# A new issue order for an H3 convolution and MLP kernel: the same operations, moved in three stretches

## The chip, the cores and the metric

The kernel runs on one core of one Trainium2 chip. The metric is the device time of one execution in microseconds (us). A core has a tensor engine (PE), a vector engine (DVE), a scalar engine (ACT), GpSimd (POOL) and a sync engine (SP). Each engine works through its own list of instructions in order and waits on semaphores for what the others deliver. SP and POOL start DMA transfers here: SP nearly all of the plain loads and stores, and POOL the transfers that add what they bring to what is already at their destination.

## What is computed

Two layers are applied twice, each on a normalised input and added back to it. Layer A is an H3 convolution, layer B a two-matrix MLP with ReLU (S = 2048, D = 640, Dff = 1728, batch 1):

```python
def A(q, k, v, shift_k, ssm_k, ssm_D):
    kv = causal_depthwise_conv4(k, shift_k) * v
    y  = irfft(rfft(pad(kv)) * rfft(pad(ssm_k)))[:S] + kv * ssm_D
    return q * y
def B(x, w1, w2):
    return maximum(x @ w1, 0) @ w2
x = q
x = x + A(layernorm(x), k, v, ...);  x = x + B(layernorm(x), w1, w2)
x = x + A(layernorm(x), k, v, ...);  x = x + B(layernorm(x), w1, w2)
```

The convolution depends on k and v alone, so both rounds multiply by the same y. The kernel computes y once, stores it in device memory (`Y`) and loads it when a gate needs it.

## The kernel before, in words

The sequence is cut into 8 chunks of 256 positions and the channels into 5 tiles of 128. A convolution **unit** `c_t` is chunk `c` of channel tile `t` (tile names carry it: `gt4_2` belongs to unit 4_2). For each unit the shift convolution is built on ACT and DVE (`tp`, `acc`), transformed blockwise on PE, and gives two spectra: `at`, that of the input, and `gt`, that of the filter. The output of a unit is a sum of products of spectra over pairs of chunks (`products`, L713): DVE multiplies `Ax` or `at` by `Gx` or `gt` into `pd` (L761) and adds it to `pacc` (L766); the sum is combined to `u` (L798 to L801), split into a high and a low half-precision part (`hlu`, L405), transformed back on PE (`pq`, L383 to L385) and stored as `Y`. Spectra that later units need are written to device memory (stores `A<-at` and `G<-gt`, L701) and loaded again as `Ax` and `Gx` (L748) into a ring of six buffers.

A spectrum has three parts; the third is the sum of the first two. From chunk 4 on that sum is made by a transfer instead of an engine: POOL starts a DMA that adds part 1 onto part 2's copy. A copy on ACT (L629 for `gt`, L670 for `at`) comes ahead of it. The same is done for the folded filter `gs` = `hf` plus or minus `hr`:

```python
def psum_(x):                                                    # L624
    plan.op("POOL", 1.1, lambda: POOL.dma_start(out=x[:, :, 2],
            in_=x[:, :, 1], accum_op=ALU.add), [x], [x], ...)    # L626
...
plan.op("POOL", 1.1, lambda g=g: POOL.dma_start(out=g.t,
        in_=hr.t, accum_op=ALU.add), [hr, g], [g], ...)          # L501
```

The text calls these forty transfers the **adding transfers**, and those of L626 a unit's **sum**. A filter's way to PE is `gs`, then its split `hlg` (L405), then the matmuls `pg` (L383 to L385).

Between the convolution's pieces runs the MLP, whose matmuls fill most of PE's time: `h` (L1319 to L1334) against the first matrix, then the split `hh` (ACT, L1470) and `hl` (DVE, L1471), then `o` and `oc` (L1303 to L1306) against the second. An `h` tile is in PSUM, and its buffer is free for the next one when `hl` has been written from it.

What is written in the program is only which operations exist and what they need. The order in which they are issued is a list, the table `ORDER` (L60 to L163): 4073 numbers packed into text, one per operation. `table` (L283) unpacks it and `issue` (L286) emits the operations in just that order; each engine's instruction list is that list cut down to its own operations. A tile takes a buffer of its ring when its first operation is issued, and waits for the buffer's last user. So the table sets three things at once: the order on each engine, the order in the DMA queues, and which buffer a tile gets.

Of the kernel before, what the change touches and what calls it, by code (L numbers as in the profile page):

```python
# [59 lines left out]
ORDER = (  # L60
    "0{{d71po#B2LK2F2>=QJ3jhoN4FC=R4*(DV5dabZ695zd6#y0h7XTOl82}mp8vq;t9RMBx9{?Z#Apjx(BLE}-B>*M>Cjck_DF7+}"
    "D*!A20st)lE&wk8FaR+CG5|9GGyquuRsdH300031Q2;dnHUKvOH~={SIsiKWJODiaJ^()eKmb7iLI6VmL;ytqMgT_uNB~IyN&rg$"
    "k^oWwTmV=ATL4S|O#n^+PXJH=S^#DMT>xnSU;thKX8>OSVE|$PmH?LkXaH&easYDxV*r={lK_+eQvjI&WB_ykbpUn%cK~<*c>sC<"
    "WdLjddjOgMn*e+OeE@y{e*l00YXFr1gaCm6f&ha6zyP5DZ2*P<ZUCGBg#g3=!2oaoB>{&3!T=`$ZvZI)D*>bcodBKyp8%i$#Q??t"
    "#{kFxaR4m=!vLZHqX4A<F99Y2hyaNIiU249tpKM0t^lt9u>hz5%K*#(&H&E<rU0@4$pDK0i~!95vjFM<sQ`@t$^fbW(Eus|ECH(k"
    "&;YmqtN_vgxd1T%GXd}bH36^y(*TYD*8q<Iv;f!u*#O%B+yFNLE&(tBG66IJ)c`pG?f}#PwE(sNI{`fbkpPeYHUZrL>;Sv~?*Q5W"
    ")&REvKLNe~;{d$?-T)8*NdXc8H~~5VK><7g;s8DY-vI3Z5dlj969E(f`~VdJO#v1G;Q&toKmkGl^8nxg<^W0o7XcmtQ31aIQvpK("
    "=Kxg!7y(xS83E`3L;?K({s2V*SpgaWTLJL^OabWtP60*%0RjI20s%(>9RWxIAps%*Z2?^YPyr(WBmsp1@&I}PZUKe?QUQkni2;fM"
    "ive%}i~(N(0|8V4Zvk-uasgHWSOJXz1OZ_IjsbH4b^-PPbODb6V*%>`djVPjTmg3hhyi>7cma6<UIAbMzX6c}x&V*?egS;}Vgd93"
    "lL5d1_W*wZ!2!DfWC6kfWdV`_#Q|mk!vSXjXaRx(!~tmmlmUPN#sO*p%K^**#{tLzl>vbPmjQzTmI2WLnE}!Pm;v<w$pM4`$^p#*"  # L70
    "r2@_Y@&Ts;fCAG2g94fXoB{Iz^a1q&)B&FX8v&aEodKZ%paG)+o&op)`2nc{_yD2-<N(hB&;j`X_5o`F_W`8=009L7qyeS@`T!*Y"
    "`T>Xn`vLm^rvV%R`~m#|*8$i8r~#<~i2@)2s{yJ32LXfv0s^c7*#X`G+5xQr+X00Fh5`ryuK}(Bs{+*l0|KxC)&aQ!hXRWN;Q`_S"
    "2?1;Y1_9gwu>pz#vH{%zi~?)|-vQtOr~<PAv;pS<=mFya<p2r+jsm&@jRFe+wE?yPj{>&=xB=w>kOH{@=>e1i3;}@xx&i6|w*uq="
    "*aGGOy8)E~mjeC)bpe(F4gtLZkpjE{k^;T~>j9Gj>;dfo?g4@U9|5KU4FT@~{{ip;00IF5m;wX>xB{vI@c{(_CIXoPCjtfnz5*x$"
    "oC2K!2m(|9tOD8s3IZttDgp-r2?DzURREd-3j(bIzyd4+Edrhb4FcQ(y#l`i3<3`VpaKvA4g#M7n*uHZ-U1N<t^zLtFaj|G!UD$v"
    "!2%Kj6ao(cp#l{G69TXT!veelD*_q<7y>c^5d*{mu>!9G76LN@qXM!5q5|py#RA&`8v+>u$pSS3HUhH(7Xrot69XOs9|AW590Ifg"
    "@dC91-vT%S$O7;J$^sn%wgMmm-2&|b%K{++&jL9D%mUd0Is(lCA_Cw7&;ro{VFc^~BLdO_;R53VKLR@fJOb_lBmzJJ<O0(I)B^7U"
    "K>{BGJp$qa{{rO#WCUgeZ31orZvr?3J_6MO&H_RLLjrID<^n|m6a(`D@&fb%>jH5Ca{_b%^#V%*Y6Kwz=K^&C=mO~ib^`VS5(9Sv"
    "cmhlUL;^+v_X0-(00RO80|QM0P69{*0Ru?_1Oqt)c>+oT6$2In{Q@=w_yQvXQ36i_QUZDc`2wQ^R0353Bm;Z`7XwoQAOjc!{sLP9"
    "83R}X1p`n5`T|)3`vP17eFD}3A_HdxB?AWoCIcq}8Uy?SegawoT>>Zr1_NRQ8v|hie*$F$2m>htJ_KR{UIJqTDg!J790OJYR{|>o"  # L80
    "2?II=LIXPl9RptiU;+vQV*+FXJOn)iEdwtD3<E<09s_6ur34EDFas_FF#}}+4Fe7XX#_+AMFU0yqylCFKLkMprvy&~Gy-b`NCQ9w"
    "X98#fX#z3>Py|N<Hv~xoGXrb{Gy`e^LIgDfHUm)vL<B_yP6Ma}QUpo^O9Mj$Mg&I$PXki~Py<l|OaoK{Hv<p@djwSjRs(GWdIUHF"
    "O#@N`O$1j1NCa8~TLY>DR0K{0R|Hc7cm!1hZUjjLIs;q-T?1hQIRjn;Vgoz_Rs>1}aspTbWCITaSpz-;d<1?3s|0TZO9VRuOayTR"
    "Km&3FWdm3QSp;wda|BuhW&>vfqy(-6c?4erfCOLzbOfdZfdqpDe*}aCV*_XdKLcq4b_6{Gf&_I0g#?BKY6FJ^*8+$Hbpv(-eFS#|"
    "sRVlhTLfGLT?DWMi3E=Xkpyc3UIdB+kOX%F#RPZ*YXfWptOR)jlLU(dj0AcEk_3$eZUdAAl>~1C_ylbOtpu?IuLR8ma077z#{@wG"
    "js$xHnFMkJngq}Ud;{A9eFL%t%LH=+vjqACfdl*mn*_!Lf&+sCgadyAfCGmE$ON1OmITZM&IJ7g{{+tjeglmIhy#TK(FD^3mju!T"
    "m;}@WkOKe(v;@fnkpr~^)daQ#h68W~i35rQjsv#@ivyknxCFTb`2@NIj{~~|z64(codlNyU<8x{l>>|e0R?mek^|NR$^-)imIK!W"
    "m;<~7+yuV_8U@${*#w^ia|N9PlLP()1qHnX`vd|7o&(+l-vplnzy!er-2~tSpabCqn*-tmoCBEyb_L@Er~|13ssrQ%cm<#YcLnAI"
    "+60;d!vwAa!UTB*uLG+Cp#!V~1O)~Kq66gw=LC8M=met$tpmgaqXV!5v;%tuA_NBo2nDqRu>%PO3I*E)=>%~F3kB)~qywb`rUQHh"
    "?gX|2as}%Iw*w3Xx&yldrvuyr4F&83r3LQ<rv<zN4h4P%e+AtG-UFcovIBGl@C3aB4+Rhfzyq@bs0FG8!vlQ<!2{m|-~)gK!~^jJ"  # L90
    "fd#1rxC6oi;sX%{xdXlf#{+@|;{&S&tOeu)$OFFv%mvB=q6EbQ#sh-|^90EQ&I9cPqy-)Y<pbse=L2;G&;t_%=mQi5hXu<6rUkAA"
    "(F5rN>jM%6gaxk!u?5Tn6$P*b>;ugM90l?O&jZo}tp(Hri3N%Uiv`mIvIX=6^#rp876pt2)dSW8hy~XJwFT`1?gNbljs=ee&IRuS"
    "g$0oX^#d0Lw*}Y(*#rLt)di3R+5_+d@dFqIk_EN}@&f?|BLwyX)CKbclLaIM^aCXXCItHf_XGF?`2(~C0R$%mDFopI0tEU4Dg=}T"
    "D+K%l%>@Gn)&&CuECjd(*98Ow1P1*B{sS!pE(8Yzh6VQo1qLq!nFR_22m}cPFa-Yt00avJ1q9gz1_llU2L>_(xdplf&jkhq5d;qe"
# [14 lines left out]
    "wg>D7(FURhDF~wm-3PY^-Uqk`xd$T%p$4c1C<x#O_y?v2rv~2#CJ3np;RpE#(gvgkzXr?(?gym?tOouEDhMkG)CT_t00^oEs|GCy"
    ";s*f;0tmVXE(p~IO$bZ~`UiIiEC~Gt(*{lm0|*2Ntp=_J1_-YPum<A?<p<;ku?7bS1qcWT3J9_WvjzzWv<5H;MhLYA3kcQ*wg%=0"  # L110
    "5C;qhdI;AB*aq1K4G0eiF9_NOd<ahnQ3w$S5(nD`69?P|PzZkr-3I#yQV1~!6bBUtG6+WqQwR<S;06!~eF)wL;s!Mc;|4Pby9c}n"
    "5eO0pSqMl7Gzc~b-v)UI;Rb;S76%jvHwYI8fC%UY<OWFydk7N<cnCNMS_o7Kp$HELRR~H5gb1k!83%$0IS4ukeh3u^<pvfA=?3No"
# [1621 lines left out]
```

## Time and profile before

| what | value |
|---|---|
| runs of the kernel before | 844.4 us median (841.74, 844.4, 845.06) |
| the profiled execution | 844.9 us, of which the span of its trace is 843.1 us |
| PE busy | 832.4 us (99%) at full granted clock in every slice |
| DVE busy | 775.8 us (92%) |
| ACT busy | 605.1 us (72%) |
| POOL busy | 45.9 us (5%) |
| plain transfers (queue q1) | 170.47 MB |
| adding transfers (queue q0) | 10.49 MB |

All times within the execution count from the start of the span. A row of the timeline gives the start, the length, the engine and line, the operation with its output and inputs, and in brackets the idle time of the engine before it and what ended that. For an instruction that only starts a transfer (DMA_DIRECT2D) the length is the time that the engine spent on starting it, waits for earlier data included; when the data landed stands in the DMA views. "PEclk" is the clock that PE was granted, 1.00 being full speed.

### The profile page before, as it was taken

How to read it: one execution, taken by the hardware profiler on the slowest of the kernel's cores; microseconds unless marked ns; L12 is line 12 of the kernel's file. 1: busy time of each engine (PE TensorE's matmuls, PEld its weight loads, DVE VectorE, ACT ScalarE, POOL GpSimd, SP SyncE). 2: the span in 40 equal slices, each digit the busy share in tenths (PEclk: the TensorE clock that was granted, in tenths of full speed). 3: DMA queues.
4: the chain of work that ended last, by engine and by line, in shares of the span. 5: the costliest groups of instructions: out<-in, count | busy, mean ns of one | idle time of the engine just before them, and what ended most of it. 6: DMA issues, size and time to landing. Idle time of an engine off the chain costs nothing.

```text
span 843.1 us, 20661 instructions
## 1 busy us (share of the span) xinstructions
PE 832.4 (99%) x8135; PEld 660.5 (78%) x8135; DVE 775.8 (92%) x1404; ACT 605.1 (72%) x1505; POOL 45.9 (5%) x58
## 2 busy tenths in 40 slices
...
GB/s 288 339 282 326 231 176 277 291 248 311 296 282 200 272 192 225 251 257 252 196 265 204 234 259 237 220 191 228 319 243 297 116 229 139 63 68 23 58 33 32
DMA packets 138435, 182.37 MB, mean 216 GB/s; under 512 B 53857, under 2 KB 95713, under 8 KB 138338
## 3 DMA queue, kind: packets, MB, share of 16 engines
q1 hardware_dynamic: 129874, 170.47, 65.8%
q0 software_dynamic: 8320, 10.49, 8.1%
...
q10 hardware_dynamic: 144, 0.10, 0.0%
...
## 4 chain that ended last, share of the span: by engine, by line
PE 84%; DVE 6%; DMA 4%; issue 3%; ACT 2%; POOL 0%; DVEq 0%; SPq 0%; POOLq 0%; ACTq 0%
PE o L1249 10%; PE h L1331 9%; PE h L1334 9%; PE h L1332 9%; PE o L1304 7%; PE o L1303 7%; PE o L1306 6%; PE h L1319 4%; DMA gt<-gt 3%; PE pg L585 2%; PE h L1321 2%; DVE pd L761 2%; PE oc L1303 2%; PE h L1364 2%; PE hs L1364 2%
## 5 line engine op out<-in xcount | busy, mean ns | idle before, releaser
L1331 PE MATMUL h<-xT,w 128*128 128x256 f16 (+1 forms) x1000 | 229.1, 249 | 0.0
L1334 PE MATMUL h<-xT,w 128*128 128x256 f16 (+1 forms) x1000 | 229.1, 249 | 0.0
L1332 PE MATMUL h<-xT,w 128*128 128x256 f16 (+1 forms) x1000 | 229.1, 249 | 0.0
L1304 PE MATMUL o<-w,hh 128*128 128x512 f16 x336 | 127.4, 379 | 0.0
L1303 PE MATMUL o<-w,hh 128*128 128x512 f16 x336 | 127.3, 379 | 0.0
L766 DVE TENSOR_TENSOR pacc<-pacc,pd 128x1536 f32<-128x1536 f32 (+1 forms) x75 | 123.1, 1641 | 0.2
L1332 PEld LDWEIGHTS <-w 128*128 128x128 f16 x1100 | 107.6, 98 | 15.2 <-issue 0.2
L1331 PEld LDWEIGHTS <-w 128*128 128x128 f16 x1100 | 107.6, 98 | 14.9 <-DVE hh L1471 0.2
L1334 PEld LDWEIGHTS <-w 128*128 128x128 f16 x1000 | 97.8, 98 | 6.4
L1303 PEld LDWEIGHTS <-hh 128*128 128x128 f16 x672 | 65.7, 98 | 26.2 <-DVE hh L1493 0.6
L1304 PEld LDWEIGHTS <-hh 128*128 128x128 f16 x672 | 65.7, 98 | 26.1
L1306 PE MATMUL o<-w,hl 128*128 128x512 f16 x208 | 78.8, 379 | 0.0
L761 DVE TENSOR_TENSOR pd<-Ax,Gx 128x768 f32<-128x768 f32 x83 | 78.0, 949 | 0.3 <-DMA Gx<-G 0.2
L1303 PE MATMUL oc<-w,hh 128*128 128x128 f16 x336 | 73.6, 219 | 0.1
L1304 PE MATMUL oc<-w,hh 128*128 128x128 f16 x336 | 73.6, 219 | 0.0
L1470 ACT ACTIVATE hh<-h 128x512 f16<-128x512 f32 (+1 forms) x97 | 46.2, 482 | 35.0 <-PE h L1334 16.7
L1306 PEld LDWEIGHTS <-hl 128*128 128x128 f16 x416 | 40.7, 98 | 26.4 <-DVE hl L1471 1.7
L1319 PE MATMUL h<-xT,w 128*128 128x256 f16 (+1 forms) x400 | 57.6, 251 | 0.0
L479 ACT ACTIVATE tp<-kt,shs 128x256 f32<-128x256 f32 (+1 forms) x78 | 43.5, 574 | 6.9 <-DVE acc L553 6.8
L1306 PE MATMUL oc<-w,hl 128*128 128x128 f16 x208 | 45.6, 219 | 1.6 <-DVE hl L1471 1.6
L761 DVE TENSOR_TENSOR pd<-at,Gx 128x768 f32<-128x768 f32 x46 | 42.9, 948 | 0.7 <-DMA at<-at 0.6
L501 POOL DMA_DIRECT2D gs<-hr x20 | 18.5, 924 | 408.2 <-DVE pacc L766 224.6
...
## 6 DMA issues: line engine op xcount, KB each, us to landing
...
G<-gt SPq DMA_DIRECT2D x14, 768.0 KB, 5.8
A<-at SPq DMA_DIRECT2D x14, 768.0 KB, 7.2
...
gs<-in_hF SPq DMA_DIRECT2D x20, 256.0 KB, 3.7
```

What stands on the lines that cost most here:

```text
L479: ACT.activation(o[:, i : i + m], kview(i, m, j), AF.Copy, scale=shs[:, t, j : j + 1])
L761: ew(f"mac{j % POOLMOD}", 768, lambda e, x=dst[i], av=av, gv=gv: e.tensor_mul(x.t, av(), gv()), [ax, gx], [dst[i]], pr_)
L766: dve(768 * (hi - lo), lambda lo=lo, hi=hi, pd=pd: DVE.tensor_add(acc[:, lo:hi], acc[:, lo:hi], pd[:, lo:hi]), [*sums[lo:hi], *dst[lo:hi]] ...
L1249: PE.matmul(b[:, c : c + w], x, y[:, z : z + w], start=done[i] == 1, stop=end, skip_group_check=fin)
L1303: PE.matmul(z, hh[:, c], wh[:, d], start=(j == JS[0] and i == 0 and (h == 0 or s == S[0])), stop=False)
L1304: PE.matmul(z, hh[:, c], wl[:, d], start=False, stop=end and tail)
L1306: PE.matmul(z, hl[:, c], wh[:, d], start=False, stop=end)
L1319: PE.matmul(p[:, z], wh, xv(t, x), start=b and x == 0, stop=e and x == 1)
L1331: PE.matmul(p[:, z], wh, xv(t, 0), start=b, stop=False)
L1332: PE.matmul(p[:, z], wh, xv(t, 1), start=False, stop=tail and e)
L1334: PE.matmul(p[:, z], wl, xv(t, 0), start=False, stop=e)
L1470: act(2 * R, lambda pv_=pv_, hh=hh: ACT.activation(hh.t, pv_(), AF.Relu), [src], [hh], URGENT)
```

## The change

Only the table `ORDER` is replaced. The operations, their sizes, their buffers and the program around them stay as they were. The diff is two pieces of packed text, of which a line shows nothing:

```diff
 ORDER = (
-    "0{{d71po#B2LK2F2>=QJ3jhoN4FC=R4*(DV5dabZ695zd6#y0h7XTOl82}mp8vq;t9RMBx9{?Z#Apjx(BLE}-B>*M>Cjck_DF7+}"
...
```

Laid against the trace of before, operations trade places in three stretches: from the start to about 200 us, from about 312 to 385 us, and from about 400 to 484 us. Elsewhere the lists are the same. On PE 782 of 1059 operations keep their place, on DVE 899 of 1330, on ACT 718 of 1130, on SP 330 of 512 and on POOL 40 of 42. No PE operation moves by more than 14 places. Rows of the lists follow; the number behind the last underscore of a name only tells tiles of one name apart.

**SP around the store of unit 4_1's `at`** (314 to 335 us of before). This store reads what the sum of `at4_1` writes, so it and all that stands behind it wait for that sum. Before:

```order
L701 DMA A4_0_142<-at4_0_5047 128x1536
L701 DMA A4_1_144<-at4_1_5624 128x1536
L465 DMA hr4_3_5951<-in_hR 128x2x256
L861 DMA Y4_74<-ys4_0_5841 128x4x128
L498 DMA gs04_3_5991<-in_hF 128x2x256
L748 DMA Gx4_2_3_2_5993<-G3_1_137 128x768
L748 DMA Ax4_2_2_2_6004<-A2_1_134 128x768
L748 DMA Gx4_2_2_2_6037<-G2_1_133 128x768
L465 DMA vt4_3_6048<-in_vT 128x2x256
L1113 DMA y3_1_00_6052<-Y2_73 128x640
L701 DMA G4_1_143<-gt4_1_5367 128x1536
```

Now:

```order
L701 DMA A4_0_142<-at4_0_5047 128x1536
L465 DMA hr4_3_5887<-in_hR 128x2x256
L1113 DMA y2_1_01_5892<-Y2_73 128x640
L748 DMA Gx4_2_3_2_5942<-G3_1_137 128x768
L465 DMA vt4_3_5964<-in_vT 128x2x256
L861 DMA Y4_74<-ys4_0_5861 128x4x128
L748 DMA Ax4_2_2_2_5998<-A2_1_134 128x768
L748 DMA Gx4_2_2_2_6056<-G2_1_133 128x768
L498 DMA gs04_3_6087<-in_hF 128x2x256
L701 DMA A4_1_144<-at4_1_5624 128x1536
L748 DMA Ax4_2_3_2_6155<-A3_1_138 128x768
L465 DMA kt4_4_6198<-in_kT 128x2x262
```

The store of `at4_1` stands eight places further back among SP's transfers; the loads of `hr4_3`, `y`, `Gx` and `vt4_3` no longer stand behind it. The next two rows now are the load of `gs14_3` and the store of `gt4_1`.

**DVE around the first products with the sum of `gt4_2`** (341.7 to 349 us of before). Before:

```order
L557 TENSOR_TENSOR acc4_3_5775<-acc4_3_5775,vt4_3_6048 128x512
L761 TENSOR_TENSOR pd4_2_2_6099<-Ax4_2_1_2_5798,Gx4_2_3_2_5993 128x768
L761 TENSOR_TENSOR pacc4_2_6101<-Ax4_2_0_2_5795,gt4_2_5959 128x768 x2
L561 TENSOR_TENSOR sd4_3_6104<-acc4_3_5775 128x256
L1479 SCALAR_TENSOR_TENSOR hl9_6_6106<-h9_6_6007,hh9_6_6081 128x256
L761 TENSOR_TENSOR pd4_2_4_6108<-Ax4_2_2_2_6004,Gx4_2_2_2_6037 128x768
L761 TENSOR_TENSOR pd4_2_2_6099<-Ax4_2_1_2_5798,gt4_2_5959 128x768
```

Now:

```order
L801 TENSOR_TENSOR u14_1_6089<-u14_1_6089,pacc4_1_5592 128x512
L761 TENSOR_TENSOR pd4_2_2_6096<-Ax4_2_1_2_5865,Gx4_2_3_2_5942 128x768
L761 TENSOR_TENSOR pd4_2_4_6098<-Ax4_2_2_2_5998,Gx4_2_2_2_6056 128x768
L761 TENSOR_TENSOR pacc4_2_6101<-Ax4_2_0_2_5789,gt4_2_5962 128x768
L1479 SCALAR_TENSOR_TENSOR hl9_6_6103<-h9_6_6016,hh9_6_6083 128x256
L761 TENSOR_TENSOR pd4_2_2_6096<-Ax4_2_1_2_5865,gt4_2_5962 128x768
L761 TENSOR_TENSOR pd4_2_4_6098<-Ax4_2_2_2_5998,Gx4_2_3_2_5942 128x768
```

A second product of loaded tiles (`pd4_2_4`) now stands ahead of the first product with `gt4_2`. Further ahead, out of these rows, `hl9_2` has gone from two operations before the pair that writes `gt4_2` (L622, L623) to four behind it, and the two `hlg` splits of unit 4_2 stand ahead of `hl9_1`.

**POOL, the last rows before the sum of `gt6_0`** (440 us of before). Before:

```order
L626 DMA gt4_4_6983<-gt4_4_6983 128x2x256
L501 DMA gs16_0_7172<-hr6_0_6920 128x512
L626 DMA at4_4_7150<-at4_4_7150 128x2x256
L501 DMA gs06_1_7463<-hr6_1_7330 128x512
L626 DMA gt6_0_7414<-gt6_0_7414 128x2x256
```

Now:

```order
L626 DMA gt4_4_6983<-gt4_4_6983 128x2x256
L501 DMA gs16_0_7129<-hr6_0_6920 128x512
L626 DMA at4_4_7157<-at4_4_7157 128x2x256
L626 DMA gt6_0_7360<-gt6_0_7360 128x2x256
L501 DMA gs06_1_7437<-hr6_1_7521 128x512
```

The sum of `gt6_0` and the addition for `gs06_1` have changed places. In the same stretch SP's load of `vt6_2` moved from behind the store of `at4_4` (L701) and the load of `Ax6_0_3_0` to ahead of both; on DVE the product of `Ax6_0_1_0` and `Gx6_0_5_0` now stands ahead of the first product with `gt6_0`. In the opening stretch the load of `hf0_0` went from first on SP to behind `kt0_2` and the two of `kt0_0`, and the store of `gt0_0` from SP's row 49 to row 67, with its reloads right behind.

More of the change, by code (lines that the diff above doesn't have):

```diff
@@ L66 @@
[L66 to L75, printed above, removed]
@@ L91 @@
-    "fd#1rxC6oi;sX%{xdXlf#{+@|;{&S&tOeu)$OFFv%mvB=q6EbQ#sh-|^90EQ&I9cPqy-)Y<pbse=L2;G&;t_%=mQi5hXu<6rUkAA"
+    "0{{d71po#B2LK2F2>=QJ3jhoN4FC=R4*(DV5dabZ695zd6#y0h7XTOl82}mp8vv33R{#J2RsdT7T>x1C0RT||S^!c2TmS+98~_~v"
+    "U;thKVE|$PSO8xD9snNzAOIl%A^;-*BmgA<CIBY@C;%w{DgY}0EC4M4E&wk8FaR+CG5|9GGypXKHUKvOH~={SV*ok;I{-WYJpeuc"
+    "KL9`gK>$JkLjaZlL;z+0MF2(sM*v6wNdQU!O8{p8X#ivZWdLdblK^M{YyeCEO#n^+PXJH=asYDxbO3b#b^vz(cmR0-dH{O>d;pgK"
+    "eE@y{e*lyKm;h4%gaDZUl>nLmYXHCi!2pH;B>{i{n*f{uodBKyfdFj)!~n$r#sGx?hX8^Ag8;_>Cjo8%Zvb!rp#X6Jp8&`J$pFd#"
@@ new lines @@
+    "!T_WIq5z-(!vH1$tpKF}qW~!ZD*=cAt^kPurvNPhr~rxpuK=+CvH-IHC;=}4rT{Sk%K(c2&Hyt3sQ|bD%mBFn&j8H;s{o7u&;Y6c"
+    "tN^e8*8tc6(E!;1+W?IKjsPkF+yJxy>HyLJ?f|s_wg9&Pj{qzI-2l@7?*KIckN~^@y#V6?E&<g5Faa_F+5j{GHUZQC-T*fNH~~2U"
+    "Isxzi)&LLzI|1wf5djhb69GK|KLPCkNdZd%;s8MbJORD{J^|kV6af|iO#$ElPXSQ@;Q&AZ`~c<v@c=>rQvnqLzW^5j7y&~8L;*zs"
+    "=l~u8839HCRRQM!Apu7L9RWxIg#rBl8UacHOabx${s1BY=>S&&SpkOuBLV*aTLFdvi2-c^Bmr&#0Rf5uive!|0s)NyT>%3DUjd8("
+    "Z~+7XdI4bpaRG7xdjVqsjsZ>qPytc_Q~_22SOHoA9079ybODF~b^(t8Tme)7cmZAkU;%dlzX4(ac>#O@WC4%?egVJ%kpaO0!U5|5"
@@ new lines @@
+    "e*t9y^8k_oW&vjblL2S}eF13!#R0<s#sT&K!~uW-#{p^ql>vhSlmW{D$N_-?_W+jx%mJ1Gm;ucJ&H>Q@(gC{wg8`WVngN6XoB{Lz"
+    "^#FhZ(*el=)B&FX$^jbzodNOzpaB2@1p)W~p#h=+o&oa#^a1q&_5q^-r2_Z?f&%ve`2m{&r2(V?`2eQ@&jHW@rvm%|`T^Gg{Q;%{"
+    "AOZRSfdcyh`v9o{r~w86hyvIFssV`t2LY=A+5zMM2mt~DtO2b7uL0Qs+W~|Et^w5n2?5~&-T|-yYXJ%Yg#uLoB?4>#ivj}zu>s!!"
+    "h60BI-~r+RvH^+$bpieX3jwnMv;pG*)&blB-2t@$rUK*v{{gxJ<pH(<w*lq>xB(0S4FS3UjsoWai~^4WjRNHWxdFQYx&e>^kpch$"
+    "y#eR}=>h5iyaB!ew*r&`sRFA4r~;A#l>+Mlz5?t4?E&rqmjc)V+5!Or?*Z@ulL7<+m;!79@d1_s1p=G`CITk{tO5oCnF6>1f&nN3"
@@ new lines @@
+    "3IZttssfz?2LdVrzyb&Yo&v1`xdJQ#paPKqEdmPy4FV1Vy#fybt^x@H4+0DVp8^pA4gs(NE&|*FngTBZFai_;p#l{Gy8_+<u>ueR"
+    "5&{teF#;0;uL7F_zXCD>76Kmu+X5>BqXNPLvH}+Z!2-hqyaJ*E8Uix{H3Ay~#{x70HUhH(!~(Sfv;xHfHv$|2I0794>H-)783M)v"
+    "9s&~s$pW?l*#h4JVFc|0-2xv1$O6g&%L2>-AOi3LAp$u9&jLCEI|4ic&;sBB%>p6<@dDujKLXJL(*ivLBLXA>;{xOYJ_0}j(gNZF"
+    "<pM<l@&auFZUXEAK?2kQZvsXFLIO(y)dC*_<^uBqZ~|lmaRNsIa{@yG&H_vV>jD%5=K}QtAp>Rv?gB&t^aB3^bOPuCbpikb?*euL"
+    "Y6La}=>m5G0s{jBBLhtWNCNf(_X2nV5(7>G6$5z!76SnTNdig&IRy9uBm?~ddIA^&Q36r|1Orn7R08<|PXbi}qyl^bSONtDSppyf"
@@ new lines @@
+    "S^|9n`T`;Y7Xw=Y1_NONVgeZh`vMvRB?Be{{sJchTmt+8egb6#8v|zqC<7}4I0Rw@2LlKLT>?-7DFapl9RpqhR{~=MLIYm{U;;V>"
+    "WddUYJOrZz90O(oDg!J7F9R(DFatgWI|K;>3Il%vLjyeoXao!cL<24ZF#}`*K?FYpdIZ)23j+-Ur35kqMFTSfKm-m0L<DIBPXuQI"
+    "XaXJsX#z$ALIg(xNCQv=QUq!OHv}{TNdr*?Qv|03Lj*+xdjw7cPXjdrYXmj}Mg&I$Oan>-Z3IgLO#@H^NCXfAcm#X|4+B&KQ3Fi`"
+    "Hv?J&I0I4xRRdH6P6TWOT?1YNIRjGzZUj~XIs;n+R|Kd8sswKYSOa+kR|81|fCO;_aspffRRnSbRs>1}egtF#I|EAuqy(k}WdnZ%"
+    "Spz-;JOf_?Oay}jVFO|Va0IIaV*_RbU;}*wX9HLSSp<XxfdqmCa|CDuS_EqXt^{fWYXd+7bOdz+h6INMJp;%DKLd6Ibp)^kTLfGL"
@@ new lines @@
+    "g#>#7hy<(zX#;Kpkpyf5T?B~)b_2x(cLR?EcmsI@cLb>fUIcFgkOYzhiUi99lmv?eu>{QoZ3C|aa08VDaRaRcdjr=3lLVOr_yl?b"
+    "d;>uPvIKGij0E}weFJ_2%mjf0a|40{`~=PfjRcMangq}Ue*=I6vjm3&{RD#pmITiP#{`4}(FB_WjRS=P(*(%`(gd6YkOR~Nkpqqc"
+    "v;>y~hy%3*#sr-Nh6B|E)&#Z$j{~;^xCDs<iUX7bivx@Ul>@m1m<0a>+ywpvU<957x&)U4*94XWy9A#E00jXB`2@TK*aUC|ode1Q"
+    "k^^4^m;=59*#rXxo&%Eu`vkuP1qI#&-vr<Uy#${FpaXLSnF9g^;RL`0cm;U{+XHb0r~|13sso?|!35$2bOW0M-2~bMas`?LqXn)5"
+    "b_I6@1_i<d!vwDb;{>Y%+XUtW<OG}pp#!1=tOI%l#02F8umk4=dj$jqu>%JMA_NEp=mhBmd<CNe2?eAB3Iz)Vv;(yR3<aeHtpn}^"
```

55 lines of the change are left out of this document (19 added, 36 removed).

## The prediction

> **What bounds the kernel now.** I read the busy times by stretch first. The columns are the stretch, its length, the busy time of PE, PEld, DVE, ACT and POOL with instruction counts, PE's clock, DMA share and GB/s.
>
> ```profile
> 2.00:100.00 98.00, 98.00 (x1019) 83.79 (x1020) 89.09 (x197) 73.79 (x169) 0.43 (x4) 1.00 0.90 299
> 100.00:200.00 100.00, 99.96 (x1178) 80.73 (x1176) 98.14 (x178) 74.90 (x203) 0.00 (x0) 1.00 0.81 261
> 340.00:360.00 20.00, 18.36 (x152) 13.02 (x150) 17.94 (x25) 15.85 (x41) 2.06 (x2) 1.00 0.96 250
> 440.00:460.00 20.00, 16.89 (x140) 11.79 (x139) 15.90 (x25) 14.23 (x37) 3.31 (x3) 1.00 0.78 210
> 460.00:660.00 200.00, 200.00 (x1687) 149.99 (x1686) 196.28 (x285) 137.33 (x344) 15.05 (x14) 1.00 0.85 238
> ```
>
> PE sets the time: from 2 us on it is full, at full clock, except for two gaps. An order list cannot shrink PE's own work, so only the gaps can be won. PE's timeline places them (start, length, what ran, idle time ahead and what ended it):
>
> ```profile
> 357.45 0.22 PE L1303 MATMUL oc<-w,hh 128*128 128x128 f16 x1
> 357.51 0.22 PE L1304 MATMUL oc<-w,hh 128*128 128x128 f16 x1
> 359.30 0.23 PE L1306 MATMUL oc<-w,hl 128*128 128x128 f16 x1 [1.57 <-DVE hl L1471]
> ...
> 452.87 0.38 PE L1304 MATMUL o<-w,hh 128*128 128x512 f16 x1
> 453.08 0.38 PE L1306 MATMUL o<-w,hl 128*128 128x512 f16 x1
> 454.27 0.27 PE L383 MATMUL pq<-hlu,cM 128*128 128x256 f16 x1 [0.80 <-ACT at L670]
> 456.84 0.27 PE L384 MATMUL pq<-hlu,cM 128*128 128x256 f16 x1 [2.30 <-DVE hlu L405]
> 456.95 0.27 PE L385 MATMUL pq<-hlu,cM 128*128 128x256 f16 x1
> ```
>
> Counted from start to start, against the pitch of the same matmuls beside them (0.06, 0.21 and 0.11 us), the first gap costs 1.79 - 0.06 = 1.73 us, the second 1.19 - 0.21 and 2.57 - 0.11, together 3.44. The sum is 5.17 us.
>
> DVE was late in both places, and its timeline says why:
>
> ```profile
> 325.55 0.96 DVE L761 TENSOR_TENSOR pd<-at,Gx 128x768 f32<-128x768 f32 x1 [0.64 <-DMA at<-at]
> ...
> 332.72 0.69 DVE L1471 SCALAR_TENSOR_TENSOR hl<-h,hh 128x512 f16<-128x512 f32 x1
> ...
> 342.31 0.95 DVE L761 TENSOR_TENSOR pd<-Ax,Gx 128x768 f32<-128x768 f32 x1
> 345.25 1.82 DVE L761 TENSOR_TENSOR pacc<-Ax,gt 128x768 f32<-128x768 f32 x2 [2.00 <-DMA gt<-gt]
> ...
> 446.19 0.67 DVE L1471 SCALAR_TENSOR_TENSOR hl<-h,hh 128x512 f16<-128x512 f32 x1
> 450.97 0.96 DVE L761 TENSOR_TENSOR pacc<-Ax,gt 128x768 f32<-128x768 f32 x1 [4.10 <-issue]
> ```
>
> It stood still for a unit's sum: 0.64 us for `at4_1`, 2.00 for `gt4_2`, 4.10 for `gt6_0` ("issue" names nothing, but the product reads `gt`). POOL's rows give the issues, the DMA views of windows that hold an issue the time to landing (last number), and the bytes by queue (q1 plain, q0 adding):
>
> ```profile
> 315.84 1.20 POOL L626 DMA_DIRECT2D at<-at  x1 [9.26 <-ACT at L670]
> 336.54 1.21 POOL L626 DMA_DIRECT2D gt<-gt  x1 [19.50 <-ACT gt L629]
> ```
>
> ```profile
> 435.65 0.92 POOL L501 DMA_DIRECT2D gs<-hr  x1 [14.20 <-DMA Ax<-A]
> 440.61 1.20 POOL L626 DMA_DIRECT2D gt<-gt  x1 [4.04 <-ACT gt L629]
> ```
>
> ```profile
> q1 hardware_dynamic: 613, 1.45, 91.7%
> ...
> gt<-gt POOLq DMA_DIRECT2D x1, 256.0 KB, 8.7
> ```
>
> ```profile
> q1 hardware_dynamic: 700, 1.31, 87.2%
> q0 software_dynamic: 12, 0.01, 1.6%
> ...
> A<-at SPq DMA_DIRECT2D x1, 768.0 KB, 8.8
> ...
> gt<-gt POOLq DMA_DIRECT2D x1, 256.0 KB, 10.3
> ```
>
> The first of these two views is 336.5 to 341 us: no byte of an adding transfer in 4.5 us, though the sum was issued at its start. The second is 440.6 to 446. Behind a plain backlog a sum thus takes 8.7 to 10.3 us. With none it takes 4.2:
>
> ```profile
> gt<-gt POOLq DMA_DIRECT2D x1, 256.0 KB, 4.2
> ```
>
> (issued at 299.76). Landing plus nothing gives the DVE starts: 336.54 + 8.7 = 345.2, 440.61 + 10.3 = 450.9.
>
> **The change part by part.** *The second wait* (-3.44). `gt6_0`'s sum now goes ahead of the addition for `gs06_1`, whose row is above; it can start some 0.6 us sooner with the ACT copy that moved up. DVE's first product with it moves back by one `pd<-Ax,Gx` (0.87 us by pitch), and without the idle time comes near 447.3 to 447.7. On SP:
>
> ```profile
> 441.79 0.38 SPq L701 DMA_DIRECT2D A<-at  x1
> 442.23 0.53 SPq L748 DMA_DIRECT2D Ax<-A  x1
> ...
> 461.92 0.49 SPq L465 DMA_DIRECT2D vt<-in_vT  x1
> ```
>
> `vt6_2` now stands ahead of these two. It takes the buffer that DVE's add of `vt6_1` hands back (it ended just ahead of the `hl` at 446.19), so the store and the load, 768 + 384 KB, leave after the time in which the sum moves. Bounds for the sum: 4.2 us alone gives 444.2; an unchanged 10.3 gives 450.3. I take about 6, landing at 446, since what stands ahead in q1 stays and what came behind goes. Then DVE never waits: 0, bound 2.6 us of DVE waiting, of which the second `hlu` has 1.2 to spare before PE reaches its `pq` (both by pitches, near 452.3 and 453.5), hence up to 1.5 on PE. I put in 0.1.
>
> *The first wait* (-1.73). Two things grow. DVE does 1.26 us more between writing `gt4_2` and its first product with the sum (9.81 us against 8.55, in pitches), and the `pq` matmuls of unit 4_1 now go ahead of the `o` at 357.51, so PE bears 1.65 us of DVE lateness there and not 0.99. Together 1.92 against 1.73: covered, by only 0.2, if the sum lands as before relative to its issue. The backlog ahead of it is the same within 0.1 MB (the store of `at4_1` comes into it, `vt`, `y` and one `Gx` leave), so 0 with a bound of 1.5 if the sum slips by as much. I put in 0.15.
>
> *The sum of `at4_1`* is what the freed SP loads run into. SP's row:
>
> ```profile
> 313.94 11.95 SPq L701 DMA_DIRECT2D A<-at  x2
> ```
>
> The row holds two stores; the second, that of `at4_1`, held SP for most of its 11.95 us, until the sum landed at 315.84 + 9.7 = 325.5. So that sum's last microseconds ran with no competitor but the store of `at4_0` (window 322.9 to 325.3):
>
> ```profile
> at<-at POOLq DMA_DIRECT2D x1, 256.0 KB, 9.7
> ```
>
> ```profile
> q0 software_dynamic: 20, 0.02, 4.5%
> q1 hardware_dynamic: 6, 0.03, 3.3%
> ```
>
> Twenty small packets beside six large ones, 0.05 MB in 2.4 us: one lagging DMA engine finishing alone. By their shares of 16 engines' 2.4 us a sum packet took 0.09 us and a plain one 0.2. Now `hr4_3`, `y`, `Gx` and `vt4_3` (about 1.2 MB) are issued from 314.4 on and share that engine's last stretch. One plain packet more between each of the last eight to ten sum packets, at 0.2 us or, smaller, at half of that, costs 0.8 to 2 us, and nothing if the lagging engine has been passed by. I take 0.8, since loads come in smaller packets than a store: landing at 326.3.
>
> PE has no room for it. `hl9_2` (332.72 before) now comes sixteen DVE instructions after the first product with `at4_1`, 11.1 us in pitches; from 325.55 it ends at 337.37. The `h` tile that takes its buffer is here:
>
> ```profile
> 337.31 0.27 PE L1331 MATMUL h<-xT,w 128*128 128x256 f16 x1
> ```
>
> So PE waits for what the sum is later than 325.5: 0.8 us, bounds 0 and 1.9. Queued behind that matmul on PE are the `o` of `hh9_2`; `gt4_2`'s matmuls are ahead and shift only if the `hlg` splits are late too (0.33 us spare).
>
> Later work shifts with PE, so nothing more is owed.
>
> *The opening* wins nothing: PE idles there only in the first 2 us and 0.04 in 100 to 200. It can lose: `gt0_0`'s store goes 18 rows back and DVE is 98% busy from 100 on. I put in 0.25 for it and for copies on ACT that now arrive just in time, bounds 0 and 1.
>
> Here the Trainium skill would have it otherwise. Its page "DMA: Bandwidth & Descriptors", section "Queues, rings and completion order", says that a DMA engine goes round the queues it has work for, packet by packet. By that a sum would start to move at once beside any backlog; the empty 4.5 us from 336.5 speak against it, while the twenty and six packets at the end agree with it. By the rule alone there would be no term for a backlog, and the sum would be 844.9 - 5.17 + 0.25 = 840.0.
>
> **Sum.** 844.9 (the profiled execution: span 843.1 and 1.8 outside) - 5.17 + 0.1 + 0.15 + 0.8 + 0.25 = 841.0 us. This execution lies 0.5 above the median of 844.4 and within the runs shown (841.74 to 845.06), so I don't shift it: 841.0, or -0.4% of the median.
>
> **The rivals.** (1) *Both waits go whole.* A sum shares packet by packet from its first microsecond, so neither the backlog nor the freed loads matter, and only the opening's 0.25 remains: 840.0. This is what the page named above would have. For it: 4.2 us alone, the interleaved tail. Against it: the empty windows. (2) *The second sum keeps its 10 us*, because the delay is set by what was queued ahead and not by the store behind it. It lands at 450.3, PE loses 1.5 again: 841.0 + 1.4 = 842.4; with the first sum also late by 1.5, 843.8, no change. For it: the store was issued 1.2 us after the sum and the sum's bytes began only near 446. (3) *Slower: the reload of `gt0_0`.* Its store, and the product that reads the reload, before:
>
> ```profile
> 43.27 0.46 SPq L701 DMA_DIRECT2D G<-gt  x1
> ...
> 80.80 0.95 DVE L761 TENSOR_TENSOR pd<-at,Gx 128x768 f32<-128x768 f32 x1
> ```
>
> Now the store is issued near 66 and the reloads right behind it, so SP stands until it lands (up to 8.8 us, as the store above) and the reload lands near 79 against a product near 81. If store and reload take 10 us more, DVE stands for about 8, and with DVE 98% busy and PE full afterwards nearly all stays: 841.0 + 8 = 849.0. It decides only once the lateness passes 2 us. For it: the store gives up 23 us of lead. Against it: 2 us are left, and DVE has 9 us idle in the first 100. (4) *The list does not do what it is for*: `gt4_2`'s and `gt6_0`'s sums behind changed traffic both land as late: that is the 843.8 of (2).
>
> **How the numbers follow.** A measurement of this kernel tells about 0.5% from no change: below 840.2 is faster, above 848.6 slower. My forecast (840.3 to 842) has 0.42, rival 1 0.27, rivals 2 and 4 0.21 (842 to 844.9), rival 3 0.10. Faster gets rival 1 and a share of the forecast's lower edge: 0.36. Slower is most of rival 3: 0.09. Within 0.5% is the rest, 0.55. The range, with every wait at its lower bound (839.7, and 0.3 for the spread of runs) to rival 2 with both waits kept and the opening's bound, is 839.4 to 844.8.
>
> **What would show it.** Right: the gap at 359.30 and those at 454.27 and 456.84 gone; DVE's wait ahead of `pacc<-Ax,gt` near 343 to 345 under 1.65 us and none near 447; `gt6_0`'s sum landing in 6 us, with the `A<-at` store issued after 446. The 0.8: the sum of `at4_1`, issued near 315.8, lands past 326, and a PE gap ahead of `h` near 337. Wrong: that sum under 9.7 us, or the one at 440 still at 10; any PE gap before 200 us; a new PE gap after 484.

## The result, and the profile after

| kernel | median, us | lowest to highest | runs |
|---|---|---|---|
| before | 844.63 | 841.74 to 846.49 | 12 |
| changed | 840.06 | 838.64 to 841.83 | 12 |

The ratio is 0.9949, with a 95% interval of 0.9937 to 0.9960: 4.6 us faster, just at the half per cent that this kernel's measurement can tell from no change. The forecast was 841.0. The profiled execution of the changed kernel took 838.6 us (span 836.9), which is the fastest of its twelve.

The stretches in which PE had its two gaps are full in that execution, but for 0.09 us (length, busy times of PE, PEld, DVE, ACT and POOL, PE's clock, DMA share, GB/s), and the only waits of PE that are left lie in the first 8 us:

```profile
340.00:360.00 20.00, 20.00 (x172) 14.81 (x171) 19.89 (x29) 16.63 (x42) 2.06 (x2) 1.00 0.92 216
440.00:460.00 20.00, 19.91 (x173) 14.96 (x171) 19.34 (x32) 17.18 (x44) 2.06 (x2) 1.00 0.89 252
...
PE spin L1579 <- POOL heps L362: 1.9, 1, 1.9
PE pg L585 <- DMA cG<-in_cG: 0.4, 1, 0.4
```

The three sums on which the prediction rests, by POOL's rows of their issues, and DVE's first product with each:

```profile
315.27 1.20 POOL L626 DMA_DIRECT2D at<-at  x1 [9.26 <-ACT at L670]
335.98 1.21 POOL L626 DMA_DIRECT2D gt<-gt  x1 [19.52 <-DVE acc L553]
436.16 1.20 POOL L626 DMA_DIRECT2D gt<-gt  x1 [12.18 <-ACT gt L629]
...
324.29 0.96 DVE L761 TENSOR_TENSOR pd<-at,Gx 128x768 f32<-128x768 f32 x1
342.78 0.95 DVE L761 TENSOR_TENSOR pacc<-Ax,gt 128x768 f32<-128x768 f32 x1
445.16 0.95 DVE L761 TENSOR_TENSOR pd<-Ax,gt 128x768 f32<-128x768 f32 x1
```

The DMA views give the times to landing (last number), in the same order:

```profile
at<-at POOLq DMA_DIRECT2D x1, 256.0 KB, 9.0
```

```profile
gt<-gt POOLq DMA_DIRECT2D x1, 256.0 KB, 6.2
```

```profile
gt<-gt POOLq DMA_DIRECT2D x1, 256.0 KB, 6.9
```

They landed at 324.3, 342.2 and 443.1: `at4_1` just in time, `gt4_2` 0.6 us and `gt6_0` 2.1 us ahead of use. Before it had been 9.7, 8.7 and 10.3 us, with DVE standing still for each.

PE was 0.56 us ahead by 122 us, in a stretch where nothing but a loss was forecast. The cause is in the rows of the dummy matmuls (`spin`) at the start, here by the microsecond; the number in the first brackets counts PE's matmuls. First the kernel before, then the changed one:

```profile
6.00:7.00 1.00, 1.00 (x12) 1.00 (x11) 0.96 (x3) 0.00 (x0) 0.00 (x0) 1.00 0.86 259
7.00:8.00 1.00, 1.00 (x15) 1.00 (x13) 0.96 (x3) 0.47 (x2) 0.00 (x0) 1.00 1.02 323
8.00:9.00 1.00, 1.00 (x22) 1.00 (x20) 0.13 (x1) 0.44 (x2) 0.00 (x0) 1.00 1.08 365
```

```profile
4.00:5.00 1.00, 1.00 (x12) 1.00 (x10) 0.00 (x0) 0.70 (x1) 0.00 (x0) 1.00 1.01 200
5.00:6.00 1.00, 1.00 (x17) 1.00 (x15) 0.00 (x0) 0.99 (x2) 0.00 (x0) 1.00 0.89 300
6.00:7.00 1.00, 1.00 (x21) 1.00 (x19) 0.48 (x2) 0.98 (x2) 0.00 (x0) 1.00 1.00 293
```

The same matmul starts every 0.107 us at first and every 0.056 us later. The switch came at 7.68 us before and at 5.55 us now, while the column of the granted clock says 1.00 throughout. Whether the list did that was a question for the experiments.

### The profile page after: what moved, and what is told of

Read it like the earlier page. It is cut to its first block, busy times and chain, and to the rows that moved or that the text cites. A ratio compares the mean times of both kernels' runs of the same rounds, so it can differ in the third digit from the quotient of the medians.

```text
span 836.9 us, 20655 instructions
## 1 busy us (share of the span) xinstructions
PE 830.6 (99%) x8135; PEld 660.0 (79%) x8135; DVE 776.4 (93%) x1404; ACT 605.8 (72%) x1506; POOL 45.9 (5%) x58
## 4 chain that ended last, share of the span: by engine, by line
PE 88%; issue 4%; DVE 4%; DMA 2%; ACT 1%; POOL 0%; SPq 0%; DVEq 0%; POOLq 0%; ACTq 0%
PE o L1249 10%; PE h L1331 9%; PE h L1334 9%; PE h L1332 9%; PE o L1303 8%; PE o L1304 8%; PE o L1306 7%; PE h L1319 4%; PE oc L1303 2%; PE oc L1304 2%; PE pg L585 2%; PE h L1321 2%; PE oc L1306 2%; PE hs L1364 2%; PE h L1364 2%
```

## The experiments

The list has three changed pieces that trade no operation with each other: up to position 1222 (the opening, to about 200 us), 1791 to 2062 (312 to 385 us, the first wait) and 2188 to 2490 (400 to 485 us, the second wait), with unchanged parts between. So pieces, and engines within a piece, can be exchanged between the old and the new list. All runs hold the same operations, but for the last, which leaves out dummy matmuls. "Stretch" below is the time between two PE matmuls that all lists hold at the same place, an `oc` at 311.29 us of before and another at 471.93; it leaves the opening out.

| run | median, us (runs) | ratio to before, 95% | `gt4_2`'s sum, us | `gt6_0`'s sum, us | stretch, us |
|---|---|---|---|---|---|
| before | 844.6 to 845.6 (12 to 29) | | 8.7 | 10.3 | 160.6 |
| changed | 840.06 (12) | 0.9949 (0.9937 to 0.9960) | 6.2 | 6.9 | 155.0 |
| change_again | 839.94 (6) | 0.9936 (0.9917 to 0.9955) | 6.5 | 5.9 | 156.6 |
| open_only | 845.28 (12) | 0.9996 (0.9978 to 1.0013) | 8.0 | 10.4 | 159.8 |
| first_only, first_only_2 | 844.25 (12), 843.56 (11) | 0.9999 (0.9982 to 1.0016), 0.9981 (0.9967 to 0.9995) | 6.0 | 10.8 | 161.2 |
| second_only | 842.25 (12) | 0.9967 (0.9954 to 0.9980) | 8.5 | 5.8 | 159.3 |
| first_sp | 844.60 (11) | 0.9993 (0.9975 to 1.0011) | 8.0 | 8.8 | 158.3 |
| first_comp | 845.13 (11) | 0.9991 (0.9975 to 1.0006) | 7.7 | 10.2 | 161.7 |
| second_sp | 840.19 (6) | 0.9938 (0.9918 to 0.9959) | 7.8 | 5.3 | 155.8 |
| second_store | 841.01 (7) | 0.9959 (0.9942 to 0.9976) | 8.2 | 7.8 | 157.0 |
| undo_store | 841.17 (6) | 0.9958 (0.9943 to 0.9972) | 6.4 | 6.7 | 156.2 |
| early_ax | 839.74 (7) | 0.9937 (0.9917 to 0.9956) | 6.4 | 6.0 | 154.7 |
| fewer_spins | 839.77 (5) | 0.9937 (0.9917 to 0.9956) | 6.7 | 7.2 | 155.9 |

The medians stand beside runs of the kernel before on the same chip (844.97 for the first four, 845.63 for the next, 845.15 for the last; second_store, undo_store, first_only_2 and fewer_spins are the last). The sums and the stretch are those of one profiled execution each; first_only itself was profiled in an execution of 3103 us, so its trace isn't read, and the sums and the stretch in its row are first_only_2's.

### One piece at a time

**open_only**: the new opening, the rest as before.

```diff
-order = before
+order = changed[0:1222] + before[1222:]
```

> The new list for the opening stretch (to 200 us) alone; the other two stretches as before. Theory 'warm-up': the 0.6 us by which the changed kernel is ahead at 122 us come from the first dummy matmuls, which ran at 0.107 us apart until 5.55 us there and until 7.68 us before, and not from the list; then the time is that of before within 0.1% (ratio 0.999 to 1.001), both waits (first 1.6 to 2, second 3 to 3.5 us on PE) stand, and the switch from 0.107 to 0.056 us comes at another moment again. Theory 'the list gains': PE is 0.5 to 0.6 us ahead at 122 us whatever the moment of the switch, ratio 0.9993. The prediction's term: 0.25 us lost, at most 1, ratio 1.0003.

Ratio 0.9996, with an interval from 0.9978 to 1.0013. The switch came at 6.72 us, a third moment, and PE was 0.5 us ahead at 122 us; but second_sp, which keeps the old opening, was 1.4 us ahead there, with the switch at 4.91. Time and trace fit the theory 'warm-up' and do not exclude a small gain by the list; no loss of 0.25 is to be seen, and no PE gap before 200 us. Over the thirteen traces the switch lies anywhere from 4.9 to 7.8 us, with the old opening (4.91, 5.02, 5.23, 6.82, 6.94, 7.68, 7.79) as with the new one (5.00, 5.54, 5.55, 5.66, 6.72, 7.37). Each microsecond of the slow phase costs half a microsecond, so with the old opening it moves an execution by up to 1.4 us. With the new one, which has 66 and not 78 dummies ahead of the first `pg`, PE waits up to 0.4 us for that matmul's data when the switch comes early, and the traces differ by 0.7 us at 200 us. At 5.0 us the new opening is thus 0.1 to 0.5 us behind the old one, at 6.8 some 0.3 ahead, each in single traces.

**first_only** and **first_only_2**: the new piece of the first wait.

```diff
-order = before
+order = before[0:1791] + changed[1791:2062] + before[2062:]
```

> The new list from about 312 to 385 us alone. Prediction's terms: gt4_2's wait on PE (1.73 us) goes, at4_1's sum lands late by 0.8 and costs PE as much: 0.8 us faster, ratio 0.9991, and a PE gap ahead of the h matmul near 337 us. Rival, from the trace of the changed kernel: at4_1's sum isn't slower (9.0 us there against 9.7), gt4_2's sum takes 6 to 7 us and not 8.7, and all 1.73 to 2.0 us are won: ratio 0.9977 to 0.998. The second wait stands in both (PE gaps of 0.8 and 2.3 us before two pq matmuls).

> The new list from 312 to 385 us alone, once more, since its profiled execution was disturbed from outside. Its time at first: 0.7 us under before. Halves: SP's order alone left gt4_2's sum at 8.0 us and a PE gap of 0.8; the other engines' order alone removed the gap but made others of 1.1 us near 365 and 393. Theory 'both are needed': together the sum takes 6.2 to 6.5 us as in the three traces of the whole change, no gap near 357 and none near 365 or 393, ratio 0.998 to 0.999. Rival: the shorter sum comes from the other stretches; then 7.5 to 8 us here, and a gap of up to 1 us remains somewhere between 355 and 395.

Medians of 0.7 and 1.6 us under before. The trace of the second has `gt4_2`'s sum at 6.0 us, no gap from 312 to 440 us, and none near 337. So by its trace the whole first wait is won by its piece alone, and `at4_1` costs PE nothing. By the time the gain is 0.4 to 2.8 us in the second run, and not told from nothing in the first. What its second wait shows is told under the last heading.

**second_only**: the new piece of the second wait.

```diff
-order = before
+order = before[0:2188] + changed[2188:2490] + before[2490:]
```

> The new list from about 400 to 485 us alone. Prediction's terms: 3.44 - 0.1 us won, ratio 0.996, gt6_0's sum lands in 6 to 7 us and DVE does not wait for it. Rival (the delay of that sum is set by what is queued ahead of it): 10 us still, DVE waits 2.6 us, ratio 0.998. The first wait stands in both.

`gt6_0`'s sum took 5.8 us and the gaps near 453 us were gone; 2.7 us were won (1.7 to 3.9 by the interval), not 3.3. The trace shows new waits. PE's longest in it:

```profile
PE oc L1306 <- DVE hl L1471: 1.0, 1, 1.0
PE pq L384 <- DVE hlu L405: 0.9, 1, 0.9
PE h L1331 <- DVE hl L1471: 0.5, 1, 0.5
```

The first is the first wait, which this kernel keeps. The two others are new: they stand at 425 and 429 us, where before had none. A wait of 0.4 us near 53, for a load of `xT`, is not from the piece.

**change_again**: the changed kernel, unaltered.

> The changed kernel once more, unaltered. If the three stretches are independent, its gain is the sum of the three others' within 0.1%. Theory 'warm-up': the profiled execution is slower than the 838.6 us seen at first by half of what its slow phase of dummy matmuls is longer (up to 1 to 1.5 us), with everything after the opening as before. Rival: the spread of 838.6 to 841.8 us comes from waits for sums that land at other moments; then this profile shows a PE gap behind 300 us.

839.94, so the result stands. The single pieces' medians add up to 3.1 to 4.0 us (-0.3 for the opening, 0.7 and 1.6 for the first wait, 2.7 for the second), less than the 5.0 of the whole here; but each has an interval of more than 1 us to both sides, so this does not show that they interact. Its trace has the switch at 5.66 us, as early as the first one, and yet the execution took 1.6 us more. The rival of this expectation was right here: two PE gaps stand behind 300 us, the same two as in second_only.

```profile
422.86 0.27 PE L384 MATMUL pq<-hlu,cM 128*128 128x256 f16 x1 [0.61 <-DVE hlu L405]
426.39 0.27 PE L1331 MATMUL h<-xT,w 128*128 128x256 f16 x1 [0.54 <-DVE hl L1471]
```

DVE is late there because it waited for the sum of `gt4_4`, unit 4_4's, which no part of the prediction mentions (DVE's row, POOL's row of the issue, time to landing):

```profile
416.08 0.96 DVE L761 TENSOR_TENSOR pd<-Ax,gt 128x768 f32<-128x768 f32 x1 [2.02 <-DMA gt<-gt]
...
408.71 1.20 POOL L626 DMA_DIRECT2D gt<-gt  x1 [3.00 <-ACT gt L629]
```

```profile
gt<-gt POOLq DMA_DIRECT2D x1, 256.0 KB, 7.3
```

In the trace of before that sum was issued at 411.91, took 4.8 us and was used at 418.44, with 1.7 us to spare:

```profile
411.91 1.20 POOL L626 DMA_DIRECT2D gt<-gt  x1 [2.96 <-ACT gt L629]
...
418.44 0.94 DVE L761 TENSOR_TENSOR pd<-Ax,gt 128x768 f32<-128x768 f32 x1
```

Now it takes 6.3 to 7.4 us in the four traces of the changed order as it stands (changed, change_again, second_only, undo_store), and DVE would come to it 5.3 to 5.5 us after the issue, not 6.5. The first trace of the changed kernel had the wait too, 0.81 us on DVE, and PE just bore it.

### The first wait: SP's order or the engines'?

**first_sp**: in that piece only SP's order is new. **first_comp**: only that of PE, DVE and ACT.

```diff
-order of SP in 1791:2062 from before      (first_sp)
+order of SP in 1791:2062 from changed
-order of PE, DVE, ACT in 1791:2062 from before      (first_comp)
+order of PE, DVE, ACT in 1791:2062 from changed
```

> Of the stretch from 312 to 385 us only SP's order is new (the store of at4_1 eight places back); every other engine keeps the order of before. Theory 'backlog': the loads that no longer stand behind that store are gone by 336 us, gt4_2's sum takes 6 to 7 us (8.0 to 8.7 in traces with the old order), DVE's first product with it waits 0 to 0.5 us and the first PE gap (0.6 to 1.6 us in the traces so far) goes. Prediction's view: the sum takes as long as before (8 to 8.7 us) because the backlog is the same, and at4_1's sum lands 0.8 us later for the new competition; the gap stays and a second one comes. Time: 0.999 or 1.001.

> The other half of the same stretch: PE, DVE and ACT in the new order, SP in the old one. Prediction's view: the sum of gt4_2 takes 8 to 8.7 us, DVE comes 1.26 us later to it and PE bears 0.66 us more, so 1.92 us cover the 1.73: DVE waits about 0.7 us, PE not at all or up to 0.3. If the rows that were moved on DVE cost PE something elsewhere (hl9_2 late for the h matmul near 337 us), a PE gap stands there. Time: 0.998 to 0.999 if all is covered, 1.000 if not.

Neither half does it. With SP's order alone the sum took 8.0 us and the gap at 357 stayed, 0.8 us (0.4 to 1.0 in the traces with the old piece, other than the first). With the engines' order alone that gap went, but PE waited 0.2 us at 365 and 0.9 at 393, the latter behind the next sum, `gt4_3`'s, which took 9.8 us. Both times lie within the interval of no change. Together the sum takes 6.0 to 6.7 us, in all six traces that hold the whole piece. In first_sp the store of `at4_1` and the load behind it were issued at 331.6 and 332.1, in change_again at 329.4 and 330.4, after a load of `Gx` that held SP for 1.5 us there and 0.4 here; and 2.15 MB of plain traffic moved while the sum was under way, against 1.35. The shorter sum thus comes from both halves. That the 0.8 MB alone make it is not shown, and first_comp speaks against it: 1.58 MB moved there and the sum took 7.7 us.

### The second wait: what stands behind the sum, or ahead of it?

**second_sp**: in the piece of the second wait only SP's order is new. **second_store**: before, with the one load of `vt6_2` moved ahead of the store. **undo_store**: the changed kernel with the store ahead of that load again.

```diff
-order of SP in 2188:2490 from before      (second_sp)
+order of SP in 2188:2490 from changed
```

```diff
 L1113 y4_0_01<-Y4                 (second_store: before, SP)
+L465 vt6_2<-in_vT
 L701 A4_4<-at4_4
 L748 Ax6_0_3_0<-A2_0
...
-L465 vt6_2<-in_vT
```

```diff
 L748 Gx6_0_4_0<-G4_0              (undo_store: changed, SP)
+L701 A4_4<-at4_4
+L748 Ax6_0_3_0<-A2_0
 L465 vt6_2<-in_vT
-L748 Ax6_0_3_0<-A2_0
-L701 A4_4<-at4_4
```

> Of the stretch from 400 to 485 us only SP's order is new (the store of at4_4 and the load of Ax6_0_3_0 behind that of vt6_2; the load of Ax4_4_3_4 earlier, ahead of gt4_4's sum). POOL still adds gs06_1 ahead of the sum of gt6_0. Theory 'what comes behind a sum slows it': gt6_0's sum takes 6 to 7 us and not 10.3, DVE's wait falls from 4.1 to under 1 us, the PE gaps near 453 us go: ratio 0.996 to 0.997. Rival 'what stands ahead decides', POOL's order among it: 9 to 10 us still, ratio 1.000. For both: gt4_4's sum takes 6 to 7.5 us (4.8 to 5.8 with the old order), but the old DVE order reaches its product 5 to 6.5 us after the issue, so little or no wait on PE there.

> The kernel before with one load moved: that of vt6_2, which SP can only issue once DVE has used the buffer (446.3 us in the first trace of before), now stands right ahead of the store of at4_4. So that store (768 KB) and the load of Ax6_0_3_0 (384 KB) leave 4 to 5 us later, behind the time in which gt6_0's sum moves; nothing that stands ahead of the sum is changed. Theory 'what comes behind a sum slows it': the sum takes 6 to 7 us and not 10.3, DVE waits under 1 us and PE 0 to 0.3 us near 453; ratio 0.9955 to 0.997. Rival 'what stands ahead decides' (the backlog and the addition for gs06_1): 9 to 10 us, the PE gaps of 3.1 us stay, ratio 0.999 to 1.001. If the late store costs later on, new PE gaps stand between 455 and 480.

> The changed kernel with only that undone: the store of at4_4 and the load of Ax6_0_3_0 stand again ahead of the load of vt6_2. POOL's swap and the new order of DVE and PE stay. Theory 'what comes behind': gt6_0's sum takes 9 to 10 us again and, issued some 1 to 1.5 us earlier and used 0.9 us later than before, makes DVE wait 1.5 to 3 us and PE 0.5 to 2: ratio to before 0.9955 to 0.998, 1 to 2 us over the changed kernel. Rival 'the swap and the later first product are what won it': 6 to 7 us, no gap, the time of the changed kernel (0.994 to 0.995).

SP's order alone wins the whole of the second wait: 5.3 us for the sum, no gap near 453, 840.19 us, which the measurement can't tell from the changed kernel. One moved load wins most of it. In second_store SP's store and load leave at 445.7 and 446.2, behind `vt6_2`, and the sum takes 7.8 us; of DVE's 4.1 us of waiting 1.6 are left, and of PE's 3.1 us 0.8:

```profile
447.43 0.96 DVE L761 TENSOR_TENSOR pacc<-Ax,gt 128x768 f32<-128x768 f32 x1 [1.62 <-issue]
...
445.24 0.38 SPq L465 DMA_DIRECT2D vt<-in_vT  x1
445.71 0.42 SPq L701 DMA_DIRECT2D A<-at  x1
446.18 0.42 SPq L748 DMA_DIRECT2D Ax<-A  x1
...
453.30 0.27 PE L384 MATMUL pq<-hlu,cM 128*128 128x256 f16 x1 [0.79 <-DVE hlu L405]
```

So plain traffic that is issued behind a sum slows it: nothing ahead of the sum was changed here, and the five traces with the old piece have 8.8 to 10.8 us. But undo_store shows that this isn't all. There the store is issued 1.4 us behind the sum again (1.2 before), and yet the sum took 6.7 us, 2.3 us ahead of its use, with 0.3 us of PE gap near 452. What had been ahead of it in POOL's queue, the addition for `gs06_1`, is now the one that waits, 9.3 us:

```profile
gt<-gt POOLq DMA_DIRECT2D x1, 256.0 KB, 6.7
gs<-hr POOLq DMA_DIRECT2D x1, 256.0 KB, 9.3
```

The changed list thus cures the second wait twice over: by SP's order, and by what undo_store keeps, POOL's swap together with the new order of PE, DVE and ACT. Which of these two does the second cure was not separated. The times agree: 841.0 and 841.2 against 840.1 and 839.9, with overlapping intervals.

### The wait that the change brought

**early_ax**: the changed kernel with one load moved. SP's order:

```diff
 L1182 xT<-xh
+L748 Ax4_4_3_4<-A3_3
 L1182 xT<-xh
 L498 gs16_0<-in_hF
-L748 Ax4_4_3_4<-A3_3
 L1182 xT<-xh
```

> The changed kernel with one load moved: Ax4_4_3_4 (384 KB) is issued ahead of a transpose that SP waits for, some 6 us earlier, when its buffer is free (402.3 us). In the changed order it is issued half a microsecond ahead of gt4_4's sum, which then takes 6.3 to 7.4 us and makes DVE wait 0.8 to 2.0 us and PE up to 1.2 near 422 to 426. Theory 'the load makes that wait': the sum takes about 5 us, DVE waits under 0.5 us, PE not at all, and the time is 0.5 to 1.2 us under the changed kernel's (ratio to before 0.993 to 0.9945). Rival 'it takes that long because of the gs load and the transposes around it': 6 to 7 us still, and the time is that of the changed kernel (0.9940 to 0.995).

The load left at 402.1 us, 5.7 ahead of the sum's issue at 407.8 instead of half a microsecond, and the sum took 5.3 us:

```profile
402.10 0.52 SPq L748 DMA_DIRECT2D Ax<-A  x1
...
413.19 0.96 DVE L761 TENSOR_TENSOR pd<-Ax,gt 128x768 f32<-128x768 f32 x1
```

DVE waits under 0.1 us, and PE nowhere behind 8 us. The stretch, 154.7 us, is the shortest of all, against 155.0 and 156.6 for the changed kernel. So without that load's new place there is no wait. But the place alone does not make it: second_sp has the load half a microsecond ahead of the sum too, the sum took 5.8 us, and DVE in its old order came 6.5 us after the issue and did not wait. It takes the load and DVE's closer product together. The median, 839.74, is 0.2 to 0.3 under the changed kernel's and its interval covers both: what the profile shows the measured time can't confirm.

**fewer_spins**: early_ax without 21 of the 96 dummy matmuls (the two loops, shortened).

```diff
-for k in range(78): PE.matmul(spin, ident16, ident16)
+for k in range(78): None if 54 <= k < 66 else PE.matmul(spin, ident16, ident16)
-for k in range(18): PE.matmul(spin, ident16, ident16)
+for k in range(18): None if k < 9 else PE.matmul(spin, ident16, ident16)
```

> The changed kernel with the early load of Ax4_4_3_4 and without 21 of the 96 dummy matmuls of the opening (12 ahead of the first pg, 9 ahead of the first pr), which compute nothing that is read. With 54 in place of 66 ahead of it PE is ready for the first pg at 6.4 to 7.7 us, whenever the spacing of the dummies falls from 0.107 to 0.056 us (4.9 to 7.7 us in the traces), and the first pg starts when its data land (7.5 to 7.9 us) in every execution. Ahead of pr the data are there at 13.1 us and PE is busy with dummies until 13.55: 0.4 us won. Expected: 0.4 to 0.9 us under early_ax, ratio to before 0.993 or less, unless DVE or ACT, busy from 100 us on, give it back (then PE gaps before 200 us).

No gain: 839.77. In its trace the switch came early, the 54 dummies were done at 6.8, and the first `pg` waited for the data of `cG`, which came at 8.0 and not at 7.5 to 7.9; 0.4, 0.8 and 0.3 us of PE gaps near 53, 454 and 473, which early_ax does not have, took more. It neither shows nor excludes the few tenths at stake.

## Why the prediction held, and which of its steps did not

- **What bounds the kernel.** Right for the profiled execution, but for 0.8 us of stalls shorter than 0.3 us each, at `oc`, `pq` and `pnu` matmuls between 352 and 416 us, which were overlooked. "Full, at full clock" does not hold for most executions, though. Of 69 executions of before that were recorded with the experiments (two above 2000 us left out), 16 have a mean granted clock of 0.999 or 1.000 and a median of 842.6 us; 53 have 0.995 to 0.998 and a median of 845.7. The forecast has no term for what these lose at a lower clock; the last section tells where two traces show it.
- **The second wait, -3.44 + 0.1.** Right in the size and in the landing (6.9 us against 6 forecast, DVE never late). The reason given, that what comes behind the sum goes, is one of two. Rival 2, a sum delayed by what was queued ahead alone, falls with second_store; undo_store leaves room for the addition for `gs06_1` as a part of the delay, not separated from the new order of the engines.
- **The first wait, -1.73 + 0.15.** Right in the outcome. The step "the backlog ahead of it is the same, so the sum lands as before" was wrong: the sum took 6.0 to 6.7 us instead of 8.7, and DVE, which by the forecast was late and left PE a cover of 0.2 us, had 0.1 to 0.75 us to spare in the six traces. The gap itself was read from its worst execution: 1.57 us in that trace, 0.4 to 1.0 in the four other traces that keep the old piece.
- **`at4_1`, +0.8.** Wrong, and by the prediction's own sign (that sum under 9.7 us): it took 9.0. A slower sum is likely all the same: 8.9 to 9.7 us, mean 9.2, in seven traces with SP's new order, against 7.9 to 9.7, mean 8.6, in six with the old one, while 2.5 to 2.8 MB and not 1.7 to 2.0 moved; the ranges overlap. But 0.8 was added to 9.7, the longest value of the old order, and PE was given no slack at all. From the usual 8.6 it lands just in time, and no trace shows a gap near 337. The term should have been about 0.
- **"Later work shifts with PE, so nothing more is owed."** This is the step that failed. The piece of the second wait also moves the load of `Ax4_4_3_4` to half a microsecond ahead of `gt4_4`'s sum and DVE's product closer behind it, and a sum with 1.7 us to spare became a wait: 0, 1.15, 1.5 and 0.5 us of PE in the traces of changed, change_again, second_only and undo_store. The forecast had a loss of about the right size in the wrong place, which is luck.
- **The opening, +0.25, and rival 3.** No loss: the reload of `gt0_0` was in time. The one gap that before does not have, 0.4 us ahead of the first `pg` (by the prediction's own list a sign of being wrong), comes with an early switch of the dummies and does not cost more than that switch wins. What the traces differ by there is the moment at which the dummies speed up.
- **Rival 1**, that a sum shares from its first microsecond: the first bytes of `gt4_2`'s sum moved 3.7 us after its issue even in the changed kernel, so it can't hold, although 840.06 lies next to its 840.0.

The sum of the steps was 3.9 us of gain, and the medians differ by 4.6. The spans of the two first traces differ by 6.2: 5.2 for the two waits, 0.5 for small stalls and 0.6 for the opening. Other traces with the old piece have narrower gaps at the first wait, most executions of before have a lower clock, and other traces of the changed order have the new wait. So 841.0 lies close to 840.06 partly by luck: it starts from an execution of 844.9 at full clock, where the median of such executions is 842.6, and has no term for the lower clock of the rest.
